# The second product of the second token group by two Strassen levels instead of one, with three weight operand sets prepared in nested units by GpSimd and VectorE

## The chip, the cores and the metric

One core of a Trainium2 chip runs the whole kernel. The metric is the device time in microseconds (us) of one execution, the median over several. The engines are TensorE (PE, with its weight loads as PEld), VectorE (DVE), ScalarE (ACT), GpSimd (POOL) and SyncE (SP), which issues most DMAs. All matrix products are in 32-bit floats.

## The reference

A block-recurrent linear attention (4 batches, 8 heads, 768 positions, head size 64) gives 3072 rows `x` of 512 numbers. A mixture of four experts follows, with all experts on all rows:

```
p = domain_probs / (domain_probs.sum(-1, keepdims=True) + 1e-09)
out = np.zeros((N, D))                      # N = 3072, D = 512
for e in range(E):                          # E = 4
    h = np.maximum(x @ w1[e], 0.0)          # w1[e]: 512 x 1024
    out += p[:, e:e + 1] * (h @ w2[e])      # w2[e]: 1024 x 512
```

## The kernel before, in words

**Units.** The rows are cut into three groups `g` of 1024 tokens. A unit is one group with one expert; there are twelve, in the order `units`: group 0 with experts 0, 1, 2, 3, group 1 with 1, 2, 3, 0, group 2 with 2, 3, 0, 1. They are counted from 0 here. The main loop (from L1691) takes the units one after another. While the second product (`h @ w2`) of unit `at` runs, the first product (`x @ w1`) of unit `at + 1` runs between its pieces.

**Slots.** Each unit is written out as 7 products times 8 slots, and `now[0]` counts the slots; slot 56 x `at` + 8 x `i` + `x` is slot `x` of product `i`. Everything on every engine is issued in this program order, and each engine works off its own queue in order. Lists of pending work (`background`, `lately`, `aside`, `own_sums`, `chores`) are drained a step at a time by the slot loop. `fits()` lets VectorE work in only while a running estimate of its queue is short.

**Strassen.** The first product always uses two levels: 7 x 7 block products of 128x128 weights with 256 columns. The second product of units 0 to 4 (`second_product`, L1108) uses one level: 7 products `SEQ2`, each four parts of four matmuls, every part followed by one VectorE instruction that scales by the gate and adds into a row tile `acc`. The second product from unit `NEST` on (`nested_product`, L1394) uses two levels: 7 products `SEQ3`, each with seven inner products of two matmuls, every inner product followed by additions into a tile `sums[m]`, which stays over units and holds the transposed result. `NEST = 2 * E - 3`, which is 5. In the trace a 32-bit matmul shows as two MATMUL instructions.

**What a nested unit needs.** Its hidden block is transposed and gated on that side: `gated` multiplies 128x512 blocks by the gate on GpSimd (`by_gate` reads `gate_bc`, which lies over the tile `decay`). `outer_sums` makes the four outer sums T1 to T4 on VectorE, and for each it first copies one operand into PSUM with ScalarE (`bring`). `inner_sums` makes four inner sums for each of the seven products on GpSimd. The weight side comes from DRAM: `prepare_w2_ops` reads `w2`, makes outer sums (`total`, `less`) and inner sums (`inner_w2`), all on GpSimd, and stores the set `w2_ops` for one expert. `feed3` loads it for the products, and `until` forces pending preparation into the queues if it is not yet issued.

**Preparation.** `chores` holds the preparation of weights for all units, in order; `pump` starts the next chore when the estimate `busy` of GpSimd's queue and of the DMAs allow. Before, the order behind unit 0 is: the sums of `w2` for expert 2, `w1` for 3, `w2` sums for 3, the `w2_ops` set of expert 2, `w1` for 0, then the sets of 3 and 0; at unit 5 the rest of `w1` for 0 is forced and the set of expert 1 joins.

**Group 1's result in two parts.** Unit 4, the first of group 1, is not nested; it leaves its result as rows in the DRAM tensor `partial`. Units 5, 6 and 7 leave theirs in `sums`, which is parked in DRAM, fetched back (`gather`), turned (`turn_rows`), added to `partial` on GpSimd and stored (`finish_rows`).

**Attention.** The attention of group 2 is put at slots 120 to about 220 (`attention`, `BEGIN`), in units 2 and 3; it uses the tile `decay` and the PSUM banks `s0` and `s1`. Behind it, at slot 221, `turn_gates` turns the gates for the nested units and writes them to DRAM (`gate_rows`).

Of the kernel before, what the change touches and what calls it, by code (L numbers as in the profile page):

```python
# [21 lines left out]
def kernel(  # L22
# [93 lines left out]
    def tt(eng, o, a, b, op):  # L116
        eng.tensor_tensor(out=o, in0=a, in1=b, op=op)  # L117
        if eng is nc.gpsimd:
            busy[0] = max(busy[0], now[0]) + math.prod(o.shape[1:]) / (640 if spare else 480)
        else:  # L120
            vector(math.prod(o.shape[1:]), PSUM in (a.space, b.space))
# [17 lines left out]
    unit_of = {u: x for x, u in enumerate(units)}  # L139
    NEST = 2 * E - 3  # L140
    FINAL = len(units) - 1
# [60 lines left out]
    def pump(pace=1.0, force=False):  # L202
        all_added(None if force else now[0])
        while results:
            results.pop(0)()
        while late and (force or late[0][0] <= now[0]):
            late.pop(0)[1]()
        begins = chores and (
            force or free[0] <= now[0] and max(moved[0], asked[0]) < now[0] + FULL and not resting[0]
            and not (packed and busy[0] > now[0] + 1)  # L210
        )
        while queue and (force or queue[0][0] <= now[0] or begins and len(queue) > LEFT):
            queue.pop(0)[1]()
        if begins:
            begin = free[0] = max(free[0], now[0] - 1)
            was = max(busy[0], now[0])
            chores.pop(0)()
            free[0] = max(free[0], begin + max(pace * (busy[0] - was), (5 if len(chores) > 13 else 7) if spare else 1))

# [47 lines left out]

    def prepare_w1(e):
        st = {}

        def block(name, i, j):
            t = stage.tile([P, 2, W], FP32, name="w1b", tag="st")
            src = moe_w1[e, j * 256:(j + 1) * 256, i * W:(i + 1) * W]
            send(out=t[:], in_=src.rearrange("(c p) f -> p c f", p=P))
            st[name] = t

        def total(name, a, b, op):
            t = stage.tile([P, 2, W], FP32, name="w1o", tag="st")
            halves(t[:], st[a][:], st[b][:], op)
            st[name] = t  # L280

        def ready(m):
            inner_w1(e, m, st[A_OF[m]])

        return weight_steps(block, total, ready)

# [37 lines left out]
    def inner_w2(e, m, blk, two):  # L324
        b = {f"A{i + 1}{j + 1}": blk[j][:, :, i * P:(i + 1) * P] for i in range(2) for j in range(2)}
        s = [x.rearrange("p c d -> p (c d)").rearrange("p (k c d) -> p k c d", k=2, c=2) for x in two("ops")]
        for name, x, y, op in S_OPS:
            b[name] = s[SLOT[name] // 2][:, SLOT[name] % 2]
            tt(nc.gpsimd, b[name], b[x], b[y], op)
        to = w2_ops[e, MS.index(m)]  # L330
        b["S3"] = s[0]
        at = (("A11", 0), ("S3", slice(1, 3)), ("A22", 3), ("S1", 4), ("A12", 5), ("S4", 6))
        store(lambda: ([send(out=to[:, x], in_=b[n]) for n, x in at], made.add(("w2", e, m))))

    def prepare_w2_ops(e, eased):
# [17 lines left out]
        def total(name, a, b, op):  # L353
            t = two("w2o")
            for q in range(2):
                tt(nc.gpsimd, t[q], st[a][q], st[b][q], op)
            st[name] = t
# [7 lines left out]
        def less():  # L365
            a, b = st["A11"], st.pop("A21")
            for q in range(2):
                tt(nc.gpsimd, b[q], a[q], b[q], ALU.subtract)
            st["S3"] = b
# [451 lines left out]
    def attention(g):  # L821

        def put(slot, f):
            steps.append((slot, f))

        for i in range(CPG):
            n, s = g * CPG + i, BEGIN[g][0] + BEGIN[g][1] * i
            put(s - 10, lambda n=n: load_more(n))
            put(s - 6, lambda n=n: load(n, "v"))
            put(s, lambda n=n: turn(n, ("s0", "s1")))  # L830
            if comes_across(n):
                put(s - 2, lambda n=n: (decayed(n), nat.pop((n, "k"))))
            put(s + (6 if comes_across(n) else 5), lambda n=n: scores(n, ("s0", "s1")))
            put(s + (12 if comes_across(n) else 10), lambda n=n: values(n, ("s0", "s1")))
            if n == NG * CPG - 1:
                put(s + 17, turn_gates)
        steps.sort(key=lambda s: s[0])
# [42 lines left out]

    def by_gate(j, at):
        n = j * 4 + (int(at[1]) - 1) * 2
        return gate_bc[:, n:n + 2].rearrange("p n t -> p (n t)").unsqueeze(1).to_broadcast([P, 2, 256])

    def gated(e, i, j, at, t):

        def step():
            x = t[:].rearrange("p (c t) -> p c t", c=2)
            tt(nc.gpsimd, x, x, by_gate(j, at), ALU.mult)
            outer[e][f"B{i + 1}{j + 1}"][at] = t  # L890

        aside.append(after(2, step))
# [3 lines left out]
    def outer_sums(e, *names):  # L896
# [5 lines left out]
        def bring(x, at, tag):  # L902
            blk = outer[e][x]
            while at not in blk:
                take(aside, True)
            there[x] = bank(tag, "hp")
            nc.scalar.copy(out=there[x][:], in_=blk[at][:])  # L907
# [71 lines left out]
    def finished(g, e, m, blocks, new):  # L979

        def later(to, a, b, order, relu=False):
# [7 lines left out]
            def step(at):  # L989
                x = there[at]  # L990
                if unit_of[g, e] >= NEST and at != order[-1]:
                    bring(order[order.index(at) + 1])
# [9 lines left out]
            blocks["left"] = 4  # L1002
            if unit_of[g, e] >= NEST:
                background.append(lambda: bring(order[0]))
# [28 lines left out]
    def first_product(g, e, m, blocks, tags):  # L1033
# [20 lines left out]
        def last(p, o):  # L1054
# [4 lines left out]
            else:  # L1059
# [3 lines left out]
                    out=o[:].rearrange("p (c t) -> p c t", c=2), in0=p[:].rearrange("p (c t) -> p c t", c=2), scalar=0.0,  # L1063
                    in1=by_gate(j, "11"), op0=ALU.max, op1=ALU.mult,
                )
# [53 lines left out]
    def second_product(g, e, m, banks):  # L1119

        def part(sj, s):
# [44 lines left out]

    partial = dram.tile([G, DOUT], FP32, name="partial")
    SEQ3 = ("M1", "M3", "M5", "M7", "M6", "M2", "M4")
# [184 lines left out]
    def first_result():  # L1353
# [19 lines left out]
        def gather(n):  # L1373
            t, po = small("y"), small("po")
            for b in range(4):
# [4 lines left out]
                )  # L1380
            send(out=po[:], in_=partial[n * P:(n + 1) * P])
            gathered_out[n] = t, po

        def turn_rows(n):
            t = gathered_out[n][0]
# [278 lines left out]

    start, w1_steps = now[0], prepare_w1(2)

    def pause_till(i, x):
# [9 lines left out]
        pause_till(2, 4), mine["M7"],  # L1677
        pause_till(3, 4), mine["M3"], *w1_steps[0:2],
        pause_till(4, 4), mine["M4"], *w1_steps[2:],
    ))  # L1680
# [6 lines left out]
    for g in range(1, NG):  # L1687
        attention(g)
    PACE = 1.0, 1.0, 1.0
    FEED = (1, 5), (2, 5)  # L1690
    first_steps = first_result()  # L1691
    for at, (g, e) in enumerate(units):
        if at == 0:
            chores.extend(prepare_w2(2) + prepare_w1(3) + prepare_w2(3))
            chores.extend(prepare_w2_ops(2, False) + prepare_w1(0))
            for x in (3, 0):
                chores.extend(prepare_w2_ops(x, True))
        ahead = units[at + 1] if at + 1 < len(units) else None
        nested, nests = at >= NEST, ahead and at + 1 >= NEST
        if at == NEST:  # L1700
            until(("w1", 0, "M4"))
            chores.extend(prepare_w2_ops(1, True))
            spare.append(True)
        if at == NEST - 1:
            forget()
            packed.append(True)
        blocks, banks = {}, {}
        for i in range(7):
            if fill2:
                feed2(*fill2.pop(0))  # L1710
# [6 lines left out]
            if nests and i == 2:  # L1717
                nc.scalar.dma_start(
                    out=gate_bc, in_=gate_rows[ahead[0] - 1, :, ahead[1]].partition_broadcast(P),
                )  # L1720
            if nested:
# [99 lines left out]
```

## Time and profile before

| what | value |
|---|---|
| median of 3 runs | 1158.05 us (1157.6 to 2179.41) |
| the profiled execution | 1158.79 us, of which the span of instructions is 1157.0 us |
| TensorE clock granted, mean | 0.997 |
| PE busy | 1143.7 us (99%), 8011 MATMUL |
| DVE busy | 788.8 us (68%) |
| ACT busy | 369.8 us (32%) |
| POOL busy | 771.7 us (67%) |
| DMA | 269.22 MB, mean 233 GB/s |

The units start at these times, read from the first matmul of each second product (L1134 or L1433): 87.7, 187.9, 295.6, 398.5, 501.4 (unit 4), 592.9 (unit 5, the first nested one), 677.5, 764.5, 850.3, 937.0, 1021.7 and 1106.4 us. The last matmul ends near 1154 us. Rows of a trace give an engine, the program's line, the operation, the tile written and the tiles read, and then busy time, mean duration, and idle time before with what ended it. L117 is the helper `tt`, through which all element-wise work of two tensors goes, so those rows are told apart by their tiles.

### The profile page before, as it was taken

What the parts mean: (1) busy time and instruction counts of PE and PEld (TensorE: products, weight loads), DVE (VectorE), ACT (ScalarE), POOL (GpSimd) and SP (SyncE); (2) the same over time, 40 slices, a digit from 0 to 9 for tenths busy, and PEclk for the clock granted to TensorE, in tenths of its full rate; (3) what the DMA queues carried; (4) which work ended last, traced back from release to release, by engine and by line L of the source; (5) the groups of instructions that cost most, each with busy time, mean ns of one, the idle gap of its engine ahead of it and who ended that gap; (6) DMA issues with size and microseconds to landing.
All of it is one profiled execution on the core that took longest, in us unless ns stands there. A gap on an engine that the chain in (4) does not pass through costs nothing.

```text
span 1157.0 us, 22155 instructions
## 1 busy us (share of the span) xinstructions
PE 1143.7 (99%) x8011; PEld 991.6 (86%) x8011; DVE 788.8 (68%) x1428; ACT 369.8 (32%) x745; POOL 771.7 (67%) x731
## 2 busy tenths in 40 slices
PE   8999999999999999999999999999999999999998
PEld 7888888888888888888888888888888888888887
DVE  3676775478477757835775567989775566676785
ACT  3422123222312321222244442343354442342332
POOL 2738318547742974873784998895995783873884
PEclk8999999999999999999999999999999999999999
DMA  8796668999899999896957667976777757657542
GB/s 189 181 276 190 185 178 243 291 295 282 264 319 311 267 304 303 264 352 180 293 189 243 185 203 252 344 225 202 220 244 247 214 175 196 196 160 215 167 191 74
DMA packets 309260, 269.22 MB, mean 233 GB/s; under 512 B 141536, under 2 KB 244128, under 8 KB 309152
## 3 DMA queue, kind: packets, MB, share of 16 engines
q1 hardware_dynamic: 290832, 262.53, 74.0%
q10 hardware_dynamic: 18320, 5.28, 2.3%
q8 instruction: 64, 1.05, 0.4%
q14 instruction: 44, 0.36, 0.1%
HBM read 194.83 MB, written 77.10 MB: 235 GB/s over the span
## 4 chain that ended last, share of the span: by engine, by line
PE 89%; DVE 5%; POOL 3%; issue 1%; DMA 1%; ACT 1%; ACTq 0%; SPq 0%; DVEq 0%; POOLq 0%
PE pg L1075 37%; PE pq L1433 20%; PE q L1134 20%; PE pM L1535 3%; DVE m L117 2%; PE pc L1535 2%; POOL acc L117 1%; PE sp L700 1%; DVE sums L117 1%; PE op L754 1%; PE op L772 1%; PE sp L707 1%; POOL ops L117 1%; DVE xs L117 1%; PE qp L670 1%
## 5 line engine op out<-in xcount | busy, mean ns | idle before, releaser
L1075 PE MATMUL pg<-xs,ws_in 128*128 128x256 f32 x1960 | 472.9, 381 | 3.1 <-DVE m L117 2.9
L1075 PEld LDWEIGHTS pg<-xs,ws_in 128*128 128x128 f32 x1960 | 368.7, 190 | 59.1 <-DVE m L117 8.9
L117 DVE TENSOR_TENSOR m<-pg,m 128x512 f32<-128x512 f32 x374 | 255.1, 686 | 102.0 <-PE pg L1075 90.4
L1134 PE MATMUL q<-w2t,m 128*128 128x256 f32 x1120 | 265.7, 380 | 0.5 <-DVE m L117 0.5
L1134 PEld LDWEIGHTS q<-w2t,m 128*128 128x128 f32 x1120 | 211.9, 190 | 30.1 <-DVE m L117 1.1
L117 POOL TENSOR_TENSOR m<-m,decay 128x512 f32<-128x512 f32 x91 | 115.6, 1284 | 89.4 <-ACT m L1092 62.8
L117 DVE TENSOR_TENSOR sums<-pq,sums 128x256 f32<-128x256 f32 x272 | 112.7, 420 | 85.7 <-PE pq L1433 77.7
L1433 PE MATMUL pq<-acc,w2t 128*128 128x256 f32 x688 | 169.2, 379 | 0.0
L1433 PEld LDWEIGHTS pq<-acc,w2t 128*128 128x128 f32 x688 | 130.5, 190 | 18.0
L1092 ACT ACTIVATE m<-m 128x512 f32<-128x512 f32 x99 | 62.4, 630 | 191.9 <-DVE m L117 189.9
L117 DVE TENSOR_TENSOR m<-m,m 128x512 f32<-128x512 f32 x112 | 100.4, 896 | 5.9 <-ACT m L1058 5.9
L1152 DVE SCALAR_TENSOR_TENSOR acc<-q,gate,acc 128x256 f32<-128x256 f32 x108 | 51.9, 480 | 75.3 <-PE q L1134 75.0
L1088 ACT COPY m<-pg 128x512 f32<-128x512 f32 x88 | 51.6, 586 | 123.8 <-PE pg L1075 122.4
L1052 ACT COPY pg<-m 128x512 f32<-128x512 f32 x77 | 45.4, 590 | 133.4 <-DVE m L117 126.2
L117 POOL TENSOR_TENSOR acc<-hT,hT 128x512 f32<-128x512 f32 x56 | 71.3, 1289 | 18.2 <-PE pq L1433 15.7
L117 POOL TENSOR_TENSOR acc<-hT,acc 128x512 f32<-128x512 f32 x56 | 71.4, 1275 | 8.5 <-PE pq L1433 4.7
L1433 PE MATMUL pq<-hT,w2t 128*128 128x256 f32 x288 | 70.0, 379 | 0.0
L117 POOL TENSOR_TENSOR w2o<-w2b 128x512 f32<-128x512 f32 x26 | 36.1, 1411 | 48.0 <-DMA w2b<-in_moe_w_dram 31.5
L1433 PEld LDWEIGHTS pq<-hT,w2t 128*128 128x128 f32 x288 | 54.5, 190 | 7.7
L1433 PE MATMUL pq<-m,w2t 128*128 128x256 f32 x228 | 55.5, 379 | 0.0
L117 POOL TENSOR_TENSOR xs<-xs 128x256 f32<-128x256 f32 x28 | 24.7, 884 | 43.3 <-DMA xs<-x_blocks 41.7
L907 ACT COPY hp<-m 128x512 f32<-128x512 f32 x84 | 48.4, 589 | 16.0 <-DVE hT L117 15.0
(145 smaller groups left out, 1443.2 us busy)
## 6 DMA issues: line engine op xcount, KB each, us to landing
w2t<-w_ops SPq DMA_DIRECT2D x129, 256.0 KB, 3.2
ws_in<-w_ops SPq DMA_DIRECT2D x40, 512.0 KB, 4.5
ws_in<-w_ops SPq DMA_DIRECT2D x60, 256.0 KB, 4.0
ws_in<-w_ops SPq DMA_DIRECT2D x40, 384.0 KB, 4.2
w2b<-in_moe_w_dram SPq DMA_DIRECT2D x56, 256.0 KB, 5.4
w_ops<-ops SPq DMA_DIRECT2D x28, 512.0 KB, 4.6
w2t<-w_sums SPq DMA_DIRECT2D x40, 256.0 KB, 4.6
w_sums<-w2o SPq DMA_DIRECT2D x16, 512.0 KB, 5.1
```

What stands on the lines that cost most here:

```text
L117: eng.tensor_tensor(out=o, in0=a, in1=b, op=op)
L670: nc.tensor.transpose(out=x[:, ac * C:(ac + 1) * C], in_=y[:, 2 * ac:2 * ac + 2].rearrange("p r d -> p (r d)"), identity=ident[:],)
L700: nc.tensor.matmul(out=sp[r][half[x], ac * BL:(ac + 1) * BL], lhsT=hc(kT)[half[r], ac, blk[x]], rhs=hc(qT)[half[r], ac, blk[x]], start=(ac ...
L907: nc.scalar.copy(out=there[x][:], in_=blk[at][:])
L1052: nc.scalar.copy(out=banks[tags[1]][:], in_=new["11"][:])
L1075: nc.tensor.matmul(out=p[:, j * 256:(j + 1) * 256], lhsT=ws[i][:, j * P:(j + 1) * P], rhs=xs[i], start=(fresh and j == 0), stop=True, skip ...
L1088: nc.scalar.copy(out=new[at][:], in_=p[:])
L1092: nc.scalar.activation(out=new[at][:], in_=new[at][:], func=AF.Relu)
L1134: nc.tensor.matmul(out=p[:, s * DH:(s + 1) * DH], lhsT=h[A_OF[m]][:, c * 256 + s * P:c * 256 + (s + 1) * P], rhs=fed2[g, e, m][uu][:, c], ...
L1152: nc.vector.scalar_tensor_tensor(out=o, in0=x, scalar=w, in1=o, op0=ALU.mult, op1=ALU.add)
L1433: nc.tensor.matmul(out=p[:, 0:256], lhsT=fed3[e, m, x // 2][:, x % 2, c * P:(c + 1) * P], rhs=b[B_OF[i]][:, c * 256:(c + 1) * 256], start= ...
L1535: nc.tensor.matmul(out=p[:, s * 256:(s + 1) * 256], lhsT=a[c][:, f:f + P], rhs=b[:, c, j * 256:(j + 1) * 256], start=(s == 0 and c == 0 an ...
```

## The change

`NEST` becomes `E`, which is 4, so unit 4 is nested as well and all of group 1 goes through `sums`. The rest of the diff makes room for that:

- `partial` is gone, with its 16 stores, 8 loads and 8 GpSimd additions.
- The gates are turned at slot 20 instead of 221. Unit 4's gates are fetched into a `stage` tile of their own (`bring_gates`), as the attention still uses `decay` then.
- For unit 4 alone, `outer_sums` and `finished` read both operands from SBUF, without the copies into PSUM, as the attention still uses `s0` and `s1`.
- The `w2_ops` set of expert 1 is made first, in place of expert 2's. Those of 2, 3 and 0 follow from slot 212 on. From slot 240 on (`spare`), VectorE makes half of their outer sums and two of four inner sums.
- The pacing changes: GpSimd's estimated cost is lower in the first units, with a factor of 1.15 in group 0, and a chore takes at least 3 slots instead of 5 or 7 once `spare` is set.
- The chores for expert 2's `w1` use two buffers of another pool and another order.

The diff, cut to its core:

```diff
-            busy[0] = max(busy[0], now[0]) + math.prod(o.shape[1:]) / (640 if spare else 480)
+            busy[0] = max(busy[0], now[0]) + math.prod(o.shape[1:]) / 640
...
-    NEST = 2 * E - 3
+    NEST = E
...
-            free[0] = max(free[0], begin + max(pace * (busy[0] - was), (5 if len(chores) > 13 else 7) if spare else 1))
+            free[0] = max(free[0], begin + max(pace * (busy[0] - was), 3 if spare else 1))
...
-    def prepare_w1(e):
+    def prepare_w1(e, first=False):
...
+            if first and name in ("A21", "A22"):
+                t = stream.tile([P, 2, W], FP32, name="w1b", tag="wb")
+            else:
+                t = stage.tile([P, 2, W], FP32, name="w1b", tag="st")
...
-            tt(nc.gpsimd, b[name], b[x], b[y], op)
+            tt(nc.vector if spare and name in ("S3", "S1") else nc.gpsimd, b[name], b[x], b[y], op)
...
-                tt(nc.gpsimd, t[q], st[a][q], st[b][q], op)
+                tt(nc.vector if spare and q else nc.gpsimd, t[q], st[a][q], st[b][q], op)
...
-                tt(nc.gpsimd, b[q], a[q], b[q], ALU.subtract)
+                tt(nc.vector if spare and q else nc.gpsimd, b[q], a[q], b[q], ALU.subtract)
...
-            if n == NG * CPG - 1:
-                put(s + 17, turn_gates)
+        if g == 1:
+            put(BEGIN[g][0] - 4, turn_gates)
...
+    def bring_gates(g, e):
+        t = gate_bc
+        if unit_of[g, e] == NEST:
+            t = gate_now[NEST] = stage.tile([P, CPG, P], FP32, name="gates", tag="st")[:]
+        nc.scalar.dma_start(out=t, in_=gate_rows[g - 1, :, e].partition_broadcast(P))
...
+            if e == NEST:
+                there[x] = blk[at]
+                return
             there[x] = bank(tag, "hp")
...
-                if unit_of[g, e] >= NEST and at != order[-1]:
+                if unit_of[g, e] > NEST and at != order[-1]:
...
-            if unit_of[g, e] in (E - 1, NEST - 1) and m in ("M2", "M6", "M5", "M3"):
-                to = rows[n] if g == 0 else partial[n % CPG * P:(n % CPG + 1) * P]
-                results.append(lambda: send(out=to[:, j * DH:(j + 1) * DH], in_=o))
+            if unit_of[g, e] == NEST - 1 and m in ("M2", "M6", "M5", "M3"):
+                results.append(lambda: send(out=rows[n][:, j * DH:(j + 1) * DH], in_=o))
...
-            send(out=po[:], in_=partial[n * P:(n + 1) * P])
-            gathered_out[n] = t, po
...
-            t, po = gathered_out.pop(n)
-            tt(nc.gpsimd, t[:], t[:], po[:], ALU.add)
-            store(lambda: send(out=rows[CPG + n], in_=t[:]))
+            send(out=rows[CPG + n], in_=gathered_out.pop(n)[:])
...
-    PACE = 1.0, 1.0, 1.0
+    PACE = 1.15, 1.0, 1.0
...
-            chores.extend(prepare_w2_ops(2, False) + prepare_w1(0))
-            for x in (3, 0):
+            chores.extend(prepare_w2_ops(1, False) + prepare_w1(0))
+            chores.append(pause_till(26, 4))
+            for x in (2, 3, 0):
                 chores.extend(prepare_w2_ops(x, True))
...
-        if at == NEST:
-            until(("w1", 0, "M4"))
-            chores.extend(prepare_w2_ops(1, True))
-            spare.append(True)
-        if at == NEST - 1:
+        if at == NEST:
             forget()
             packed.append(True)
         for i in range(7):
+            if (at, i) == (NEST, 2):
+                until(("w1", 0, "M4"))
+                spare.append(True)
...
-            resting[0] = at == NEST - 1 and i >= 5 or at == NEST and i == 0
+            resting[0] = at == NEST - 1 and i == 6
...
-                    if nested or nests:
+                    if nested or nests and not steps and not lately:
                         rest()
```

More of the change, by code (lines that the diff above doesn't have):

```diff
@@ L266, in weight_steps @@
         ]
-    def prepare_w1(e):
+    def prepare_w1(e, first=False):
         st = {}
         def block(name, i, j):
-            t = stage.tile([P, 2, W], FP32, name="w1b", tag="st")
+            if first and name in ("A21", "A22"):
+                t = stream.tile([P, 2, W], FP32, name="w1b", tag="wb")
+            else:
+                t = stage.tile([P, 2, W], FP32, name="w1b", tag="st")
             src = moe_w1[e, j * 256:(j + 1) * 256, i * W:(i + 1) * W]
@@ L283, in ready @@
             inner_w1(e, m, st[A_OF[m]])
+        if first:
+            return [
+                lambda: (block("A11", 0, 0), block("A21", 1, 0), block("A22", 1, 1)), pause(4),
+                lambda: total("S1", "A21", "A22", ALU.add), lambda: ready("M4"),
+                lambda: total("S3", "A11", "A21", ALU.subtract), lambda: ready("M1"), lambda: ready("M5"),
+                lambda: (block("A12", 0, 1), total("S2", "S1", "A11", ALU.subtract)), lambda: ready("M6"),
+                lambda: ready("M2"), lambda: ready("M7"),
+                lambda: total("S4", "A12", "S2", ALU.subtract), lambda: ready("M3"),
+            ]
         return weight_steps(block, total, ready)
@@ L879, with by_gate @@
     within = {}
-    def by_gate(j, at):
+    gate_now = {}
+    def bring_gates(g, e):
[3 more added lines that the diff above has]
+        nc.scalar.dma_start(out=t, in_=gate_rows[g - 1, :, e].partition_broadcast(P))
+    def by_gate(e, j, at):
         n = j * 4 + (int(at[1]) - 1) * 2
-        return gate_bc[:, n:n + 2].rearrange("p n t -> p (n t)").unsqueeze(1).to_broadcast([P, 2, 256])
+        return gate_now.get(e, gate_bc)[:, n:n + 2].rearrange("p n t -> p (n t)").unsqueeze(1).to_broadcast([P, 2, 256])
     def gated(e, i, j, at, t):
@@ L888, in step @@
             x = t[:].rearrange("p (c t) -> p c t", c=2)
-            tt(nc.gpsimd, x, x, by_gate(j, at), ALU.mult)
+            tt(nc.gpsimd, x, x, by_gate(e, j, at), ALU.mult)
             outer[e][f"B{i + 1}{j + 1}"][at] = t
@@ L1002, in later @@
             blocks["left"] = 4
-            if unit_of[g, e] >= NEST:
+            if unit_of[g, e] > NEST:
                 background.append(lambda: bring(order[0]))
@@ L1063, in last @@
                     out=o[:].rearrange("p (c t) -> p c t", c=2), in0=p[:].rearrange("p (c t) -> p c t", c=2), scalar=0.0,
-                    in1=by_gate(j, "11"), op0=ALU.max, op1=ALU.mult,
+                    in1=by_gate(unit_of[g, e], j, "11"), op0=ALU.max, op1=ALU.mult,
                 )
@@ L1164, in second_product @@
         return [lambda sj=sj, s=s: part(sj, s) for s in range(2) for sj in (1, 0)] + [done]
-    partial = dram.tile([G, DOUT], FP32, name="partial")
     SEQ3 = ("M1", "M3", "M5", "M7", "M6", "M2", "M4")
@@ L1373, in gather @@
         def gather(n):
-            t, po = small("y"), small("po")
+            t = gathered_out[n] = small("y")
             for b in range(4):
@@ L1380, in gather @@
                 )
-            send(out=po[:], in_=partial[n * P:(n + 1) * P])
-            gathered_out[n] = t, po
         def turn_rows(n):
-            t = gathered_out[n][0]
+            t = gathered_out[n]
             nc.vector.transpose(out=t[:], in_=t[:])
@@ L1663 @@
             trickle()
-    start, w1_steps = now[0], prepare_w1(2)
+    start, w1_steps = now[0], prepare_w1(2, True)
     def pause_till(i, x):
@@ L1677 @@
         pause_till(2, 4), mine["M7"],
-        pause_till(3, 4), mine["M3"], *w1_steps[0:2],
-        pause_till(4, 4), mine["M4"], *w1_steps[2:],
+        pause_till(3, 4), mine["M3"], *w1_steps[0:4],
+        pause_till(4, 4), mine["M4"], *w1_steps[4:],
     ))
@@ L1717 @@
             if nests and i == 2:
-                nc.scalar.dma_start(
-                    out=gate_bc, in_=gate_rows[ahead[0] - 1, :, ahead[1]].partition_broadcast(P),
-                )
+                bring_gates(*ahead)
             if nested:
```

## The prediction, made before the changed kernel ran

> **What bounds the kernel now.** I read the page first: busy shares, then the chain that ended last.
>
> ```profile
> span 1157.0 us, 22155 instructions
> PE 1143.7 (99%) x8011; PEld 991.6 (86%) x8011; DVE 788.8 (68%) x1428; ACT 369.8 (32%) x745; POOL 771.7 (67%) x731
> PE 89%; DVE 5%; POOL 3%; issue 1%; DMA 1%; ACT 1%; ACTq 0%; SPq 0%; DVEq 0%; POOLq 0%
> ```
>
> TensorE is the chain, so only two things can change the time: fewer matmuls, or longer waits of TensorE for somebody else. The price of a matmul comes from the starts in the timeline of TensorE in unit 4 (start, busy us, what):
>
> ```profile
> 503.09 1.89 PE L1075 MATMUL pg<-xs,ws_in 128*128 128x256 f32 x8
> 504.82 1.89 PE L1134 MATMUL q<-w2t,m 128*128 128x256 f32 x8
> 506.54 1.89 PE L1075 MATMUL pg<-xs,ws_in 128*128 128x256 f32 x8
> ```
>
> Eight MATMULs start every 1.725 us, so one costs 0.2157 us, in both products. The 379 to 381 ns that the groups show overlap and are no price. Next I cut the trace at the unit starts (columns: stretch, length, then busy us of PE, PEld, DVE, ACT, POOL, clock, DMA share, GB/s):
>
> ```profile
> 398.52:501.36 102.84, 102.60 (x966) 88.20 (x965) 70.40 (x125) 24.32 (x56) 76.03 (x89) 1.00 0.94 294
> 501.36:592.86 91.50, 90.96 (x421) 79.63 (x420) 57.87 (x90) 26.15 (x46) 56.24 (x57) 1.00 0.81 259
> 592.86:677.54 84.68, 84.68 (x394) 74.39 (x392) 47.43 (x83) 38.82 (x80) 65.29 (x59) 1.00 0.66 204
> 677.54:764.49 86.95, 85.88 (x393) 73.98 (x392) 71.18 (x129) 29.29 (x53) 75.72 (x68) 1.00 0.86 274
> 764.49:850.32 85.83, 85.47 (x393) 74.00 (x392) 68.90 (x127) 31.43 (x56) 68.42 (x64) 1.00 0.71 221
> 850.32:937.01 86.69, 85.36 (x393) 74.06 (x392) 53.22 (x93) 41.53 (x86) 65.07 (x56) 1.00 0.71 221
> 937.01:1021.69 84.68, 84.68 (x393) 74.40 (x392) 60.28 (x114) 29.42 (x53) 55.25 (x45) 1.00 0.63 186
> ```
>
> These are units 3 to 9. A nested unit that waits for nothing takes 84.68 us (units 5, 9). Units 6, 7 and 8 lose 2.27, 1.15 and 2.01 us, 5.4 together, and the waits of TensorE in 592.86 to 937 us say to whom:
>
> ```profile
> PE pg L1075 <- DVE m L117: 2.6, 7, 0.7
> ```
>
> VectorE comes too late with the eviction that frees a PSUM bank. At DVE 56% (unit 5) and 71% (unit 9) nothing is lost, at 80% (unit 7) 1.15 us, at 82% (unit 6) 2.27 us.
>
> **What is removed.** Unit 4's second product has 7 x 4 x 4 matmuls, 224 MATMULs; nested it has 7 x 7 x 2, 196. That is 28 x 0.2157 = **6.04 us** off the chain. The trace confirms the size: unit 4 takes 91.50 us, unit 5 takes 84.68; of the 6.82 between them 0.8 is unit 4's own waiting. All else that goes lay beside TensorE and is worth nothing: 28 scalings on VectorE (13.5 us in unit 4), 16 stores and 8 loads of `partial`, 8 additions on GpSimd (10.2 us, in units that end on TensorE). The last unit's joining and storing is untouched.
>
> **Unit 3.** It now makes unit 4's gated block while the attention of group 2 still runs. VectorE gains 12 of the 16 outer sums, which read both operands from SBUF, and three gated evictions (0.69 us each, 2.1), and loses three sums of the old form. GpSimd gains up to 13 gate products and 4 inner sums at 1.27 us, 21.6 us, on 76.0 of 102.84: 95% if nothing else moves, less as the faster pacing takes chores forward. The price of a two-SBUF sum on VectorE is in the rows by tile (count, ns min/median/max), against one with an operand in PSUM:
>
> ```profile
> L117 DVE TENSOR_TENSOR m<-m,m x13: 675/1241/1814, 502.6 to 582.7; 128x512 f32<-128x512 f32 x13
> L117 DVE TENSOR_TENSOR hT<-hp,m x56: 677/681/693, 587.6 to 1118.2; 128x512 f32<-128x512 f32 x56
> ```
>
> The same work takes 0.68 us flat with one operand in PSUM, and 0.68 to 1.81 with both in SBUF. With unit 3's mean of 0.86 or unit 4's of 1.18 the net addition (9 sums and the evictions) is 9.8 to 12.7 us, so 80 to 83 of 102.84, at most 81%. Nearest rows: units 9 (71%, nothing) and 7 (80%, 1.15). I take +0.5, bounds 0 and 2.3. The gates' fetch stands on ScalarE's queue and may wait there for a `stage` buffer, with ScalarE's evictions behind it: a store from such a buffer lands in 4.6 us, so 0 to 4.6; I take 0, as a matmul needs those evictions only a slot later and the chores pause soon after.
>
> **The operand sets.** One set is 28 inner sums at 0.73 us and 8 half outer sums at 1.28 on GpSimd, 30.7 us. Expert 1's set takes the place of expert 2's: that one was through on GpSimd at 439 us, and the nested product asks for its set at about 488, so it hides. Sets 2, 3 and 0 fall from slot 212 to about 365, into units 4, 5 and the first part of 6. VectorE takes 14 inner and 4 half sums of each, all two-SBUF. Nearest rows: `xs<-xs` 128x256, 0.90 us in units 6 and 7 (free 0.41), and the 1.18 above: 14 x 0.90 + 4 x 1.18 = 17.3 us a set; free it would be 8.4; with every one at the longest seen (1.75 and 1.81) 31.7. Loads of VectorE then:
> - Unit 4 looks as unit 5 does now: 47.4 + 17.3 = 64.7 of 84.68, 76%. Between rows at 71% and 80%: +0.5.
> - Unit 5 adds to `sums` on VectorE where ScalarE copied before: 47.4 + 28 x 0.42 + 17.3 = 76.5, 90%. No row is that high; the nearest is unit 6: +2.2.
> - Unit 6 has its 71.2 and 0.6 of a set, 81.6: 94%. It loses 2.27 already; +0.8.
> - Units 7 and 8 lose GpSimd's set work (23 and 11 us there now), and with it what their two-SBUF sums collide with: -1.0 of the 3.2 they lose, bounds 0 and -2.
>
> Together +2.5. Bounds: in unit 5 the longest prices leave 90.9 us of work in 84.68, +6.2; in unit 6 90.2, +3.3 over now; in unit 4 79, no overflow, unit 7's 1.2: +10.7. Downward, free prices put unit 5 at 80% (+1.1); if half of unit 6's waits go with GpSimd's half of the set (-1.1) and units 7 and 8 gain 2, it is -2.0.
>
> The Trainium skill speaks against this change: "SBUF — State Buffer", section "Who interferes with whom", says that a VectorE instruction with two SBUF inputs contends with a GpSimd instruction that reads SBUF, and that the loser blocks for that whole instruction. The two rows above agree: the excess reaches 1.13 us, near one GpSimd 128x512 of 1.28. By the rule alone each of 18 sums a set could stand a full 1.28 longer, 23 us on the free 8.4, which is 31.4.
>
> **Queues.** `turn_gates` moves by 200 slots; its transpose (0.27 us), a copy and a DMA go along, past attention that needs none of them. `finish_rows` stores straight behind the turning, so SP waits there for a 0.70 us transpose with weight loads behind it; they are asked for units ahead. Both nothing; SP waits today up to 5.0 us for `pg` with TensorE full, so that is its upper price.
>
> **Sum.** -6.04 + 0.5 + 2.5 = -3.0. The profiled execution took 1158.79 (span 1157.0 and 1.8 around it), so 1155.8; the median of the runs is 0.74 lower: **1155.0 us**.
>
> **Rivals.**
> - *VectorE gives it all back* (20 in 100). The two-SBUF sums meet GpSimd nearly every time: -6.04 + 10.7 + 2.3 = +7.0, 1165. For: the median of 1241 ns in unit 4 lies halfway to the worst. Against: 26 such sums in unit 3, at POOL 74%, cost 0.86 in the mean. It decides from VectorE at about 95% in unit 5.
> - *GpSimd comes late in unit 4* (6 in 100, the slower side). `until` at slot 240 forces what is left of `w1` for expert 0 ahead of the inner sums, and TensorE waits for those. All of it is 28 x 0.73 + 8 x 1.28 = 30.7 us, and with expert 1's set still open 61.4; less the lead of the inner sums, one product (12.1 us): -6 + 18.6 = +12.6 (1170.7) or +43 (1201). It decides once the backlog exceeds 12.1 us. Against: before, that chore ended at 510.2 us, slot 230, with the slower pace.
> - *The waits go as well* (8 in 100). Half sets on GpSimd also free units 6 to 8: -6.04 - 5.4, 1146.6. Against: unit 8's two largest waits lie in bursts on VectorE that adds `sums<-sums,jp`, which the change leaves.
>
> **Numbers.** The forecast holds with 66 in 100; its own range is 1150 (-6.04 - 2) to 1160 (half the bounds up). The range 1150 to 1166 takes in the first rival and leaves out the other two. A measurement of this kernel tells about 2% from no change, 23 us. Faster by that needs more than the 6.04 and all 13.3 us in which TensorE idles now: 0.01. Slower by that: most of the second rival and a tail of the first, 0.07. Within: 0.92.
>
> **What would show it.** Right: 7983 MATMULs; unit 4 near 85 us; DVE 85% and more in units 5 and 6, and TensorE's waits there 'pg <- DVE m'; `ops` rows on DVE well over 0.41 us. Wrong: waits of TensorE for POOL `acc` in unit 4 (second rival), units 5 and 6 at 84.7 (third), unit 3 longer than 104, or a wait for `w2t` loads.

## The result and the profile after

| | before | after |
|---|---|---|
| median | 1158.84 us of 4 runs (1157.6 to 2179.41) | 1171.66 us of 4 runs (1170.52 to 1177.29) |
| profiled execution | 1158.79 us, span 1157.0 | 1171.51 us, span 1169.7 |

The change made the kernel slower by 1.2%: the ratio is 1.0124, 95% interval 1.0082 to 1.0166. Ratios leave out two runs that took far longer than the others of the same kernel, 2179.41 us of the kernel before and 1845.78 of e5 below; without them the medians are 1158.05 and 1174.48. The page of the changed kernel, lines of the span, of the engines and of the chain:

```profile
span 1169.7 us, 22184 instructions
PE 1143.4 (98%) x7983; PEld 986.6 (84%) x7983; DVE 832.2 (71%) x1502; ACT 368.6 (32%) x742; POOL 785.1 (67%) x714
PE 47%; DVE 5%; DMA 1%; issue 1%; SPq 0%; ACT 0%; DVEq 0%; ACTq 0%
```

The 28 MATMULs are gone, 8011 to 7983, and PE is still as busy as before (busy time counts the slow matmuls shown below in full). The chain names TensorE for 47% only, since it can be followed back no further than to 524 us. Cut at the first matmul of each second product, units 3 to 6 of the changed kernel are (columns as before: stretch, length, then busy us of PE, PEld, DVE, ACT, POOL, clock, DMA share, GB/s):

```profile
400.43:512.72 112.29, 105.09 (x966) 89.62 (x965) 75.78 (x127) 23.20 (x53) 83.47 (x87) 0.97 0.86 267
512.72:601.91 89.19, 86.36 (x393) 73.94 (x392) 63.88 (x99) 35.10 (x73) 79.39 (x68) 1.00 0.82 263
601.91:687.94 86.03, 85.38 (x394) 74.03 (x393) 67.76 (x131) 29.38 (x53) 68.22 (x61) 1.00 0.83 261
687.94:776.77 88.83, 86.86 (x393) 73.62 (x392) 78.94 (x144) 29.36 (x52) 69.83 (x59) 1.00 0.84 267
```

| unit | before | after | difference |
|---|---|---|---|
| all ahead of unit 3 | 398.5 | 400.4 | +1.9 |
| 3 | 102.85 | 112.29 | +9.4 |
| 4 | 91.50 | 89.19 | -2.3 |
| 5 | 84.68 | 86.03 | +1.35 |
| 6 | 86.95 | 88.83 | +1.9 |
| 7 to 10 | 341.87 | 341.88 | 0 |
| 11 | 50.60 | 51.02 | +0.4 |

The sum is +12.7, as the spans say. The large row is unit 3, whose matmuls did not change; unit 4 saved little more than a third of the 6.04 that its matmuls give. (In the experiments below other than e3, which paces the first units differently, unit 3 starts between 397.5 and 402.8 us, though their code is nearly the same up to there; I read nothing from the +1.9.)

Where unit 3 loses: the waits of TensorE over the whole of the changed kernel (what waited, for what, us in total, times, longest), and then its timeline at the longest of them.

```profile
PE pg L1098 <- DVE m L117: 7.3, 12, 1.5
PE sp L719 <- POOL kn L117: 6.7, 2, 5.7
```

```profile
479.60 0.69 PE L712 MATMUL sp<-qx,kx 64*64 64x64 f32 x32
485.99 1.12 PE L719 MATMUL sp<-vn,kn 64*64 64x64 f32 x16 [5.70 <-POOL kn L117]
487.04 3.52 PE L1098 MATMUL pg<-xs,ws_in 128*128 128x256 f32 x8
490.40 1.89 PE L1157 MATMUL q<-w2t,m 128*128 128x256 f32 x8
```

TensorE stands 5.70 us in the attention of the last chunk until GpSimd has decayed `kn`. The eight MATMULs of `pg` behind the wait then need 3.36 us (487.04 to 490.40) instead of 1.73, another 1.6, and the attention's own sixteen in between 1.05 (485.99 to 487.04; 0.56 in e1, where nothing held them up), another 0.5. With the 1.5 us for a late eviction at 510.88 these are 9.3 of the 9.4.

GpSimd's own timeline shows why `kn` is late; of the changed kernel, and below it of the kernel before:

```profile
460.19 2.50 POOL L117 TENSOR_TENSOR w1o<-w1o,w1b 128x512 f32<-128x512 f32 x2 [7.00 <-DMA w_ops<-ops]
...
480.78 1.71 POOL L117 TENSOR_TENSOR m<-m,gates 128x512 f32<-128x512 f32 x1
482.45 2.48 POOL L117 TENSOR_TENSOR w1o<-w1b,w1o 128x512 f32<-128x512 f32 x2
484.89 1.05 POOL L117 TENSOR_TENSOR kn<-kn,decay 128x512 f32<-128x512 f32 x1
```

```profile
467.05 1.05 POOL L117 TENSOR_TENSOR kn<-kn,decay 128x512 f32<-128x512 f32 x1
468.06 1.86 POOL L117 TENSOR_TENSOR ops<-w1b 128x256 f32<-128x256 f32 x2
```

Before, `kn` ran first, 68.5 us into the unit, and the sums of `w1` for expert 0 behind it. After, it runs 84.5 us into the unit: those sums (paced faster) and gate products stand ahead of it, and GpSimd has stood 7.00 us for a `stage` buffer that was still being stored, of which the gates now hold one. From 460 to 509 us it has no gap. The waits of GpSimd in unit 3, before and after:

```profile
POOL xs L117 <- DMA xs<-x_blocks: 20.6, 4, 10.5
POOL w1o L117 <- DMA w_ops<-ops: 3.2, 1, 3.2
```

```profile
POOL xs L117 <- DMA xs<-x_blocks: 19.8, 4, 9.9
POOL w1o L117 <- DMA w_ops<-ops: 7.0, 1, 7.0
POOL m L117 <- ACT m L1115: 1.9, 1, 1.9
```

The prediction did not count these waits: 76.03 us busy and 23.8 us of standing make 99.8 of 102.84. GpSimd was all but full in unit 3 already, and after it is again: 83.47 busy and 28.7 of standing are 112.2 of 112.29.

### The profile page after: what moved, and what is told of

Its sections match the earlier page's. It is cut to its first block, busy times and chain, and to the rows that moved or that the text cites. A ratio compares the mean times of both kernels' runs of the same rounds, so it can differ in the third digit from the quotient of the medians.

```text
span 1169.7 us, 22184 instructions
## 1 busy us (share of the span) xinstructions
PE 1143.4 (98%) x7983; PEld 986.6 (84%) x7983; DVE 832.2 (71%) x1502; ACT 368.6 (32%) x742; POOL 785.1 (67%) x714
## 3 DMA queue, kind: packets, MB, share of 16 engines
q8 instruction: 64, 1.05, 0.4%
## 4 chain that ended last, share of the span: by engine, by line
PE 47%; DVE 5%; DMA 1%; issue 1%; SPq 0%; ACT 0%; DVEq 0%; ACTq 0%
PE pq L1450 23%; PE pg L1098 23%; DVE m L117 2%; DVE sums L117 1%; DMA w_ops<-ops 1%; DVE hT L117 1%; DVE xs L117 1%; DVE w2o L117 1%; SPq L114 0%; PE pg L1450 0%; PE pM L1321 0%; DMA xs<-x_blocks 0%; DMA w2t<-w_ops 0%; PE yp L1281 0%; DMA w_ops<-w2b 0%
## 5 line engine op out<-in xcount | busy, mean ns | idle before, releaser
L1157 PE MATMUL q<-w2t,m 128*128 128x256 f32 x896 | 212.5, 380 | 0.0
L1450 PE MATMUL pq<-acc,w2t 128*128 128x256 f32 x800 | 196.9, 379 | 0.0
L117 DVE TENSOR_TENSOR sums<-pq,sums 128x256 f32<-128x256 f32 x321 | 132.4, 420 | 87.8 <-PE pq L1450 77.7
L1157 PEld LDWEIGHTS q<-w2t,m 128*128 128x128 f32 x896 | 169.7, 190 | 23.2
L1450 PEld LDWEIGHTS pq<-acc,w2t 128*128 128x128 f32 x800 | 151.9, 190 | 20.7
L117 POOL TENSOR_TENSOR acc<-hT,acc 128x512 f32<-128x512 f32 x64 | 82.8, 1294 | 11.3 <-PE pq L1450 6.2
L117 DVE TENSOR_TENSOR m<-m,m 128x512 f32<-128x512 f32 x96 | 86.2, 898 | 4.7 <-ACT m L1081 4.7
L1450 PE MATMUL pq<-hT,w2t 128*128 128x256 f32 x336 | 82.4, 380 | 1.1 <-DVE sums L117 1.1
L117 POOL TENSOR_TENSOR acc<-m,acc 128x512 f32<-128x512 f32 x44 | 57.2, 1300 | 3.4
L1450 PEld LDWEIGHTS pq<-m,w2t 128*128 128x128 f32 x264 | 49.6, 190 | 8.8 <-DVE sums L117 2.3
```

Source lines behind the costliest of these rows:

```text
L1157: nc.tensor.matmul(out=p[:, s * DH:(s + 1) * DH], lhsT=h[A_OF[m]][:, c * 256 + s * P:c * 256 + (s + 1) * P], rhs=fed2[g, e, m][uu][:, c], ...
L1450: nc.tensor.matmul(out=p[:, 0:256], lhsT=fed3[e, m, x // 2][:, x % 2, c * P:(c + 1) * P], rhs=b[B_OF[i]][:, c * 256:(c + 1) * 256], start= ...
```

## The experiments

Theory after this reading: GpSimd's queue runs some 15 to 20 us late in the second half of unit 3, and whoever needs it next holds TensorE; on top of that, the sums with two SBUF operands and VectorE's share of the sets cost in units 4 to 6. Rivals: the wait is only an order (`kn` behind two chores); it is the transfers; it is VectorE. All edits are against the changed kernel, and lengths of units come from the profiled executions.

**e1: `kn` of the last chunk five slots earlier.**

```diff
-                put(s - 2, lambda n=n: (decayed(n), nat.pop((n, "k"))))
+                put(s - (7 if n == NG * CPG - 1 else 2), lambda n=n: (decayed(n), nat.pop((n, "k"))))
```

> The key decay of the last attention chunk (GpSimd, kn<-kn,decay) is issued at slot 197 instead of 202; nothing else changes. Theory A (GpSimd's queue in unit 3 is late, and the scores' matmuls sp<-vn,kn wait 5.7 us for it, after which TensorE runs 8 matmuls at half the clock, 1.7 us): the wait is gone, unit 3 takes about 105 us instead of 112.3, the profiled execution about 1164 instead of 1171.5. Theory B (TensorE waits there for VectorE's two-SBUF sums, and kn is only the last to arrive): unit 3 stays at 110 or more and the time within 2 us of 1171.5.

1169.94 us, ratio to before 1.0091 (1.0062 to 1.0119). `kn` is in time, yet unit 3 still takes 110.70. TensorE in e1:

```profile
486.83 3.62 PE L1098 MATMUL pg<-xs,ws_in 128*128 128x256 f32 x8 [2.50 <-DVE m L117]
...
506.10 2.71 PE L1098 MATMUL pg<-xs,ws_in 128*128 128x256 f32 x8 [3.13 <-DVE m L117]
```

and what VectorE itself waited for just before each:

```profile
484.98 0.42 DVE L117 TENSOR_TENSOR kv<-kv,sp 128x256 f32<-128x256 f32 x1 [2.72 <-POOL kv L117]
...
503.71 1.73 DVE L117 TENSOR_TENSOR hT<-m,m 128x512 f32<-128x512 f32 x1 [2.81 <-POOL m L117]
```

The wait moved on to the next two who need GpSimd: the decay of the attention's state, then a gate product. VectorE stands there with TensorE's evictions queued behind. The order of `kn` alone is not the cause.

**e2: unit 4's outer sums by PSUM again.** One operand is copied to PSUM as for the other nested units.

```diff
-            if e == NEST:
-                there[x] = blk[at]
-                return
             there[x] = bank(tag, "hp")
```

> Unit 4's 16 outer sums get one operand through PSUM by a ScalarE copy, as in the later units (16 copies of 0.59 us more on ScalarE). Theory A says nothing changes before 500 us: the kn wait of 5.7 us stays. Theory B (hT<-m,m of 1.1 to 1.7 us are blocked by GpSimd and delay the evictions): these sums take 0.68 us, TensorE's wait of 1.5 us at 511 us and most of the 3 us that unit 4 waits for DVE m go, unit 4 about 86 instead of 89.2, in all -4.5 us, 1167. If the sums are not at fault: 1171.5, or more by ScalarE's copies.

1166.37 us, 1.0064 (1.0039 to 1.0089). Unit 4 falls from 89.19 to 86.80, unit 3 stays (112.17). The rows by tile of VectorE between 400 and 610 us (ns min/median/max), in the changed kernel and in e2:

```profile
L117 DVE TENSOR_TENSOR hT<-m,m x8: 676/1426/1739, 505.7 to 525.2; 128x512 f32<-128x512 f32 x8
L117 DVE TENSOR_TENSOR hT<-m,hT x8: 683/1208/1751, 515.7 to 535.4; 128x512 f32<-128x512 f32 x8
```

```profile
L117 DVE TENSOR_TENSOR hT<-hp,m x16: 674/681/692, 505.2 to 609.3; 128x512 f32<-128x512 f32 x16
L117 DVE TENSOR_TENSOR hT<-hp,hT x12: 681/681/692, 513.1 to 609.9; 128x512 f32<-128x512 f32 x12
```

The 16 sums take 0.68 to 1.75 us with two SBUF operands beside a full GpSimd, and 0.67 to 0.69 with one operand in PSUM; TensorE paid 2.4 us for it in unit 4. (The second pair of rows also holds 12 sums of unit 5.)

**e4: no share of the sets for VectorE.** The three sums with `nc.vector if spare ...` go back to GpSimd.

```diff
-            tt(nc.vector if spare and name in ("S3", "S1") else nc.gpsimd, b[name], b[x], b[y], op)
+            tt(nc.gpsimd, b[name], b[x], b[y], op)
...
-                tt(nc.vector if spare and q else nc.gpsimd, t[q], st[a][q], st[b][q], op)
+                tt(nc.gpsimd, t[q], st[a][q], st[b][q], op)
...
-                tt(nc.vector if spare and q else nc.gpsimd, b[q], a[q], b[q], ALU.subtract)
+                tt(nc.gpsimd, b[q], a[q], b[q], ALU.subtract)
```

> VectorE's share of the three operand sets goes back to GpSimd (15 us a set). Theory C (the sets' two-SBUF work on VectorE makes units 5 and 6 wait): unit 5 from 86.0 to 84.9, unit 6 from 88.8 to 87, unit 4 down by 1, in all -4 us, 1167.5. Rival: GpSimd then has 52 + 30.7 us of work in 84.7 us a unit and TensorE waits for acc or for w2t, 1172 or more. The kn wait of 5.7 us in unit 3 stays in either case.

1165.99 us (9 runs), 1.0058 (1.004 to 1.0077). Unit 4 87.62 (-1.6), unit 5 84.68 (-1.35, nothing left), unit 6 86.12 (-2.7). GpSimd could carry the sets alone in these units; giving half of them to VectorE only cost. Unit 3 stays slow, 110.81, with a 4.3 us wait for `kn`.

**e3: the old pace.**

```diff
-            busy[0] = max(busy[0], now[0]) + math.prod(o.shape[1:]) / 640
+            busy[0] = max(busy[0], now[0]) + math.prod(o.shape[1:]) / (640 if spare else 480)
...
-    PACE = 1.15, 1.0, 1.0
+    PACE = 1.0, 1.0, 1.0
```

> The estimate of GpSimd's cost and the factor of group 0 are those of before (480 until spare, 1.0); all else is the change. If the faster pacing put the w1 sums of expert 0 in front of kn: kn comes in time, unit 3 near 105, but more of w1 for expert 0 is left to be forced at slot 240, so unit 4 waits for GpSimd acc by up to 10 us. If the kn wait comes from the gate products and the stage buffer that the gates take: a kn wait of 3 us or more stays. Total 1164 to 1174.

1237.2 us, 1.0676 (1.0647 to 1.0704). Unit 3 takes 122.58, unit 4 95.81, unit 5 104.06, units 6 and 7 97.66 and 98.51. TensorE's longest waits:

```profile
PE pg L1098 <- DVE m L117: 26.6, 11, 17.9
PE pq L1450 <- issue: 22.8, 3, 8.8
PE pq L1450 <- POOL ops L117: 5.7, 2, 4.6
```

The 17.9 is VectorE standing 17.57 us for a gate product. The later waits, put down to `ops` or to nothing that the profile shows ("issue"), fall where SP is still storing parts of a set (`w_ops<-ops`); I take them for waits for sets that are not made in time, which no run tested. So the faster pace is needed, and this is the price of a GpSimd that comes late in earnest: my second rival's mechanism, from unit 3 on. One thing came as expected: `kn` runs at 478.48, ahead of the sums of `w1` for expert 0 (479.50) as before the change, and TensorE does not wait for it in unit 3. So it was the faster pace that had put those sums ahead of it.

**e5: the inner sums of `x` asked for six slots later**, so that GpSimd does not stand for their transfers. **e7: the same with the edits of e2 and e4.**

```diff
-            chores.insert(0, lambda: x_inner(g, m))
+            late.append((now[0] + 6, lambda: chores.insert(0, lambda: x_inner(g, m))))
```

> The GpSimd sums on the fetched blocks of group 1 (xs<-xs, four for each of seven products) are put in its queue 6 slots after their DMA is issued, not at once. In the change GpSimd stands still 19.8 us in unit 3 waiting for those DMAs (x_blocks) at the head of its queue. Theory A2 (GpSimd's whole queue runs late in unit 3, so that key decay, state pass and gate products all come late, and curing one moves the wait to the next): those stops go from 19.8 to under 8 us, the kn wait of 5.7 us goes and no other takes its place, unit 3 from 112.3 to 106 or less, profiled 1165 or less. Rival A1 (it is the work that the change adds on GpSimd in unit 3, not the stops): unit 3 stays at 110 or more.

> The x sums 6 slots later, the outer sums of unit 4 by PSUM and the operand sets all on GpSimd, together. If the three causes add: unit 3 105, unit 4 85.5, unit 5 84.7, unit 6 86.1, total 1157.0 - 6.0 + 2 + 1 - 0.8 = 1153 of span, 1155 us, below the kernel before. If the sets on GpSimd make it late again: unit 4 and 5 wait for acc, 1160 or more.

1174.48 us (three runs), 1.016 (1.0138 to 1.0182), and 1170.64, 1.0108 (1.0086 to 1.0131): unit 3 grew to 118.56 and 119.09. The standing for `xs` fell from 19.8 to 5.9 us, but that for a `stage` buffer rose to 15.1 in e5:

```profile
POOL w1o L117 <- DMA w_ops<-ops: 15.1, 2, 11.2
POOL kn L117 <- DVE acc L1175: 8.6, 1, 8.6
POOL xs L117 <- DMA xs<-x_blocks: 5.9, 2, 5.4
```

GpSimd now waits for buffers instead, and `kn` has waits of its own. That edit failed; the standing of the queue was exchanged, not removed.

**e6: the gate products of unit 4 left out.** The blocks of unit 4 stay ungated; everything else is done.

```diff
-            tt(nc.gpsimd, x, x, by_gate(e, j, at), ALU.mult)
+            if e != NEST:
+                tt(nc.gpsimd, x, x, by_gate(e, j, at), ALU.mult)
```

> The 13 gate products of unit 4 on GpSimd are left out, so part of group 1's expert 1 is not weighted by its gate. That takes 16.5 us of GpSimd off units 3 and 4. Rival A1 (added work): three of them stand ahead of kn, 4.7 us, so the kn wait falls from 5.7 to about 1; the rest stand ahead of the outer sums, so the 1.5 us at 511 go; unit 3 at 104 to 105, profiled 1163. Theory A2 (stops at DMAs) allows a part of it: unit 3 106 to 110.

1167.11 us, 1.0081 (1.0063 to 1.0099). Unit 3 falls to 104.35, with one wait in it:

```profile
PE sp L719 <- POOL kn L117: 1.5, 1, 1.5
```

GpSimd still stands 7.1 us for the buffer and 20.5 for `xs`; 13 products fewer on its queue are enough. `kn` needs none of these products, and the wait for it fell by 4.2 us, near the 4.7 expected of the three that stood ahead of it: for `kn` it is the added work that decides, on a queue that its stops had filled. The late eviction is gone too, but the edit takes away both the work and VectorE's need for its result, so it does not tell which of them cost that. The whole does not show the 8 us: unit 1 took 111.28 here, with a 2.4 us wait for another `kn` (that unit takes from 107.6 to 111.3 in kernels that do the same in it), and unit 6 89.94. Unit 4 stays at 89.49, so the gate products are not what costs there.

**e8: the gates of unit 4 in two tiles of their own** in place of a `stage` buffer, which are filled by two DMAs.

```diff
-            t = gate_now[NEST] = stage.tile([P, CPG, P], FP32, name="gates", tag="st")[:]
+            gate_now[NEST] = [small("gates")[:].rearrange("p (n t) -> p n t", t=P) for _ in range(2)]
...
+                nc.scalar.dma_start(out=t, in_=gate_rows[g - 1, 4 * j:4 * j + 4, e].partition_broadcast(P))
```

> Unit 4's gates lie in two of the 42 small tiles instead of one of the seven stage buffers that the chores share. Theory A3 (GpSimd stands 7.0 us at the sum S2 of w1 for expert 0, as its stage buffer is still being stored; the gates have taken a buffer away, and kn and the gate products stand behind that): the stop falls from 7.0 to 3.2 us, as it was before, or less, kn comes in time or at most 2 us late, unit 3 from 112.3 to 104 to 106, profiled 1162 to 1164. Rival A1 (the 21 us of added gate products and inner sums alone): the stop goes but unit 3 stays at 110 or more.

1168.5 us, 1.0098 (1.0083 to 1.0114). The stop for the buffer is gone (7.0 to 0), and with it the wait for `kn` in unit 3. The unit takes 108.30, more than the 104 to 106 expected; what is left there is one wait:

```profile
PE pg L1100 <- DVE m L117: 4.0, 1, 4.0
```

**e9 (e8 with e2 and e4) and e10 (e2 with e4).**

> The gates in small tiles, the outer sums by PSUM and the operand sets all on GpSimd, together. If they add: unit 3 105, unit 4 85.5, unit 5 84.7, unit 6 86.1, span 1157.0 + 2 - 6 - 0.8 + 1 = 1153, about 1155 us, below the kernel before. If unit 3 keeps its wait: 1160.

> The outer sums by PSUM and the operand sets all on GpSimd, the gates as in the change. If the two add: units 4 to 6 as in the run before this (85.5, 84.7, 86.1), unit 3 at 110 as in each of them alone, profiled 1158 to 1160. If the sets on GpSimd need VectorE's slack: nothing beyond either alone, 1162 to 1166.

e9: 1159.24 us (10 runs), 1.0023 (1.0006 to 1.004); e10: 1163.3, 1.0057 (1.004 to 1.0073). Units 4 and 5 are at 85.24 and 84.67 in e10: all but 0.6 of unit 4's loss was the two edits, 2.4 and 1.6. Unit 3 is 111.22 in e10 and 108.05 in e9. What is left of it in e9, on ScalarE and then on TensorE:

```profile
504.86 1.11 ACT L929 COPY hp<-m 128x512 f32<-128x512 f32 x2 [4.23 <-POOL m L117]
```

```profile
506.82 3.01 PE L1097 MATMUL pg<-xs,ws_in 128*128 128x256 f32 x8 [3.27 <-DVE m L117]
```

The copy for an outer sum waits for the last gated blocks, which stand on GpSimd behind four inner sums (498.4 to 503.6 us); VectorE waits for the copy with an eviction behind it.

**e11: e9 with unit 4's outer sums issued six slots later. e12: e11 with the last `kn` two slots earlier.**

```diff
-        background.extend(after(4 + 2 * (i > 4), lambda fs=fs: [f() for f in fs]) for i, fs in enumerate(work))
+        background.extend(after((10 if e == NEST else 4) + 2 * (i > 4), lambda fs=fs: [f() for f in fs]) for i, fs in enumerate(work))
```

```diff
-                put(s - 2, lambda n=n: (decayed(n), nat.pop((n, "k"))))
+                put(s - (4 if n == NG * CPG - 1 else 2), lambda n=n: (decayed(n), nat.pop((n, "k"))))
```

> As e9 (gates in tiles of their own, outer sums by PSUM, sets on GpSimd), with the outer sums of unit 4's hidden block issued six slots (about 11 us) later. Theory (the last wait of unit 3 in e9, 3.3 us and some 1.7 us at half clock behind it, comes because VectorE stands 4 us for a gate product with evictions queued behind it; six slots later GpSimd has done the gating): unit 3 falls from 108.05 to about 104, unit 4 stays near 86, the whole at 1154 to 1156. Rival (GpSimd's lateness only moves on: the inner sums that follow are then late for the second product of unit 4): unit 3 falls, unit 4 grows by as much, the whole stays at 1159, or gets longer.

> As e11, with the last kn<-kn,decay of the attention issued two slots (about 3.5 us) earlier. Theory (each stall is the next consumer of GpSimd's late queue, and kn's is the last small one, 0.75 us in e9): unit 3 another 0 to 1 us shorter than in e11, the whole within 1 us of e11. Rival (moving kn ahead makes the state's decay or a gate product late, as in e1): unit 3 1 to 3 us longer than in e11, with a wait of VectorE for kv<-kv,decay or of ScalarE's copy for a gate product.

e11: 1155.64 us (12 runs), 0.9989 (0.9974 to 1.0005). e12: 1154.36 us (12 runs) beside 1157.67 of before, 0.997 (0.9956 to 0.9983): faster than both kernels, though by little. Units 3 to 6 of e12:

```profile
399.57:502.22 102.65, 102.49 (x966) 88.16 (x965) 73.08 (x123) 23.21 (x53) 82.20 (x86) 1.00 0.93 287
502.22:587.44 85.22, 84.88 (x394) 74.40 (x393) 49.96 (x86) 41.30 (x85) 81.93 (x80) 1.00 0.83 259
587.44:672.11 84.67, 84.67 (x394) 74.39 (x393) 58.68 (x111) 29.32 (x53) 82.19 (x79) 1.00 0.85 270
672.11:758.44 86.33, 85.56 (x394) 73.81 (x393) 70.43 (x129) 29.29 (x52) 82.91 (x77) 1.00 0.90 281
```

Unit 3 is back at 102.65, and TensorE waits 0.2 us in it, with GpSimd busy 82.20 and standing 21.0 for `xs`, which fills the unit. Its work is nearly the same (83.47 in the changed kernel): the 7 us of standing for a buffer went, and those who wait for the late results were moved. In units 4 to 6 GpSimd is busy 96 to 97% and costs TensorE nothing in unit 5. Unit 4 is 6.28 below that of before. e11's unit 3 took 103.34, 0.5 of it a wait for `kn` that e12 does not have; unlike in e1, nothing behind the earlier `kn` came late. The medians of e11 and e12 are too close to tell more.

## Why the prediction was wrong

**The bottleneck and the gain were right.** TensorE is the chain, the MATMULs are 7983, and freed of its waits unit 4 gives the 6.04 that I had priced (6.28 in e12).

**The step that failed is unit 3.** I wrote of GpSimd "95% if nothing else moves, less as the faster pacing takes chores forward" and priced only VectorE's part: +0.5, bounds 0 and 2.3. It cost 9.4. GpSimd's load was not too low: 12 gate products (1.53 us in the mean, not 1.27) and 4 inner sums came in, other chores had gone forward, and it was busy 83.47 us, not 97.6. But I took a share of busy time for a price, and by that share there was room. The 23.8 us of standing in the kernel before left 3.0 us. Nor did the faster pacing help here: it put chores ahead of `kn` (e3 undoes that). That the gates take one of the `stage` buffers I saw as a question for ScalarE's queue ("I take 0"); the one that paid was GpSimd, 7.00 us instead of 3.2, and TensorE behind it. e8 shows this part and e6 the load; e9, e11 and e12 remove the rest by moving who waits.

My second rival was this mechanism, a GpSimd that comes late, but I looked for it in unit 4, on the inner sums, and set its point at the backlog of `w1`. In unit 4 TensorE waits for no `acc`. That its price of +12.6, 1170.7 us, lies beside the measured 1171.66 is luck: it was worked out from another backlog in another unit. The test that I listed, "unit 3 longer than 104", was the one that told.

**Unit 4: -5.5 forecast, -2.3 measured.** Two terms of it were misplaced. I put 12 of the 16 outer sums into unit 3; 4 began there and 12 in unit 4. All 16 took 1.33 us in the mean, and with one operand in PSUM unit 4 is 2.4 us shorter (e2). VectorE's share of the sets cost 1.6 there (e4) where I had 0.5. At DVE 72% over the unit that seems too much, by my scale of 71% for nothing; but the mean hides a burst: VectorE is busy 84% from 512.72 to 536 us, where the outer sums run, and 67% in the rest of the unit.

**Sized off.** Unit 5: +2.2 forecast, +1.35 measured, all of it the share (e4 undoes it). DVE reached 79%, not 90%: the 128x256 sums of the sets (`ops`, 40 of them) took 0.48 us in the mean, 0.42 in the median, where I had 0.90 from `xs<-xs`. The 128x512 sums of the sets on VectorE, 10 of them, took 1.32 in the mean where I had 1.18. Unit 6: +0.8 forecast, +1.9 measured, at 89%. Units 7 and 8: -1.0 forecast, 0 measured, though GpSimd's busy time there fell by 16.6 and 13.5 us, so its set work had not been what they wait for. The condition of the first rival (two-SBUF sums that meet GpSimd nearly every time) held for the 128x512 sums, unit 4's and the sets', but not for the 128x256 ones.

**Sum of the misses.** Unit 3 +8.9, unit 4 +3.2, unit 5 -0.9, unit 6 +1.1, units 7 and 8 +1.0, outside these +2.3: 15.6 on top of the forecast -3.0 is +12.6 (12.7 by the spans; the terms are rounded).

## What to carry to other kernels

Before loading an engine that works off its queue in order, add its waits to its busy time, stretch by stretch: time in front of a transfer need not be free for other work. Then look for who reads its late results soonest, above all an engine that has other work for the critical one queued behind. Moving that consumer some slots back, with all the work left in, brought unit 3 from 108.05 to 103.34 (e11 against e9); taking the 13 gate products off brought it from 112.29 to 104.35 (e6). Moving the producer's one late result forward only handed the wait to the next in e1; in e12, with the other waits cured, it handed it to nobody.

## What the runs showed of the hardware

**A short pause of TensorE can cost more than itself.** The granted clock in 5 us stretches around the pause of the changed kernel:

```profile
481.00:486.00 5.00, 0.01 (x2) 0.01 (x2) 0.36 (x1) 0.63 (x1) 5.00 (x5) 0.73 0.70 230
486.00:491.00 5.00, 5.00 (x27) 4.18 (x28) 1.09 (x2) 0.00 (x0) 4.76 (x8) 0.58 0.27 106
491.00:496.00 5.00, 4.99 (x23) 4.07 (x23) 4.63 (x9) 1.75 (x3) 4.92 (x5) 1.00 0.98 332
```

After 5.70 us of waiting, a MATMUL starts every 0.43 us instead of 0.2157. The Trainium skill, "TensorE: Matmul & The Clock Gate", in Part 1 on the clock gate, gives an idle window of about 3.4 us, after which the clock is halved, and about as long a busy one until it is full. For the busy one this case is near: slow matmuls for 4.4 us here, 485.99 to 490.40, and for 3.5 in e1, 486.83 to 490.29. The idle one is no safe bound: in e1 the pause was only 2.50 us, and the clock behind it was

```profile
487.00:489.00 2.00, 2.00 (x5) 1.63 (x6) 1.57 (x4) 0.43 (x1) 1.92 (x2) 0.50 0.94 295
```

The pauses of 3.13 us (e1) and 3.27 (e9) were followed by slow matmuls too; the 1.5 us one in the changed kernel was not. But the length of the pause alone does not decide. The same wait, for a `kn` in unit 1, in e10 and then in e6, each with the eight matmuls behind it:

```profile
232.56 0.69 PE L719 MATMUL sp<-vn,kn 64*64 64x64 f32 x32 [2.42 <-POOL kn L117]
233.18 1.99 PE L1154 MATMUL q<-w2t,m 128*128 128x256 f32 x8
```

```profile
232.90 0.69 PE L719 MATMUL sp<-vn,kn 64*64 64x64 f32 x32 [2.38 <-POOL kn L117]
233.53 3.67 PE L1158 MATMUL q<-w2t,m 128*128 128x256 f32 x8
```

After 2.42 us they run at the full clock, after 2.38 us at half of it. A pause of 2.69 us in e5, which ends at 465.00, was followed by the full clock as well. What decides between these no run here shows.

**Two SBUF operands beside GpSimd.** In the changed kernel the 16 outer sums of unit 4 (128x512) took 1.33 us in the mean instead of 0.68, and all but one of them ran beside a busy GpSimd. The 128x256 sums of the sets took 0.42 in the median, nearly the free 0.41, for they hardly met it: GpSimd's own sums of the same set need VectorE's and stood still for them, 19.2 us in 12 waits. Of the 40 sums, 34 met no GpSimd instruction, or one for 0.02 us, and took 0.41 to 0.43 us; the other six took 0.42 to 1.49.
